# A sketch load moved to GpSimd's queue, set-up reordered, and one idle matmul removed, in a polysketch attention and GELU kernel

## Chip, cores and metric

The kernel runs on one core of a Trainium2 chip. The metric is the device time of one execution in microseconds (us). Times inside the execution are counted from the start of the profiled span. The engines are PE (matrix products, with PEld for its weight loads), DVE, ACT and POOL (GpSimd); SP only issues DMAs.

## What is computed

Attention with a polynomial sketch as its feature map, and then a two-layer block with an exact GELU over all 4352 tokens (4 batches of 1088, 4 heads of 32 channels):

```python
def phi(x):
    a = np.einsum('rd,bhsd->bhsr', S1, x)
    b = np.einsum('rd,bhsd->bhsr', S2, x)
    return np.einsum('bhsi,bhsj->bhsij', a, b).reshape(*x.shape[:-1], r * r)
q_p, k_p = (phi(q), phi(k))
kv = np.einsum('bhsf,bhsd->bhfd', k_p, v)
z = np.sum(k_p, axis=2)
num = np.einsum('bhsf,bhfd->bhsd', q_p, kv)
den = np.einsum('bhsf,bhf->bhs', q_p, z)[..., None] + 1e-06
attn_out = (num / den).astype(np.float32)
...
h = x @ w_in
g = 0.5 * h * (1.0 + erf(h * inv_sqrt2))
return (g @ w_out).astype(np.float32)
```

S1 and S2 are the two sketch matrices, 8 x 32 each. They arrive as float64, as the two weight matrices do, and are rounded to float32 on the chip: a 64-bit number is loaded as two 32-bit words, and a chain of small DVE and ACT operations puts them together.

## The kernel before

The work has two stages. The head, about the first 23 us, computes the attention of the first batch and prepares the first pieces of the weights. From there on the block's two layers run over nine chunks of tokens (eight of 512, and one of the 64 tokens left over of each batch), with the attention of the later batches woven in between. PE carries that second stage.

The order is written out by hand. A loop at the end of the text (lines 1122 to 1128) ties each instruction to the one before it on the same engine, so every engine executes in the order of the source. What an engine does early in the text it does early in time, and an instruction that waits holds up all that follow on its engine.

The steps at the start that matter here:

- **Loads of the sketches.** Lines 187 to 189 issue two DMAs from ACT's queue, S1 and then S2, into the upper and the lower half of one small tile, raw_SR (16 rows). Line 190 then loads ACT's activation table.
- **Other loads.** SP issues, in this order, the keys of batch 0 in two halves (line 192: heads 0 and 2, then 1 and 3), the first queries (193), the values in two halves (195), remainders (197) and the first weights (198 to 200).
- **Set-up on POOL.** Lines 222 to 226 and 235, 236: the identity (make_identity, two operations), a mask for the heads (mask4), a bias (below), and constants for the values' remainder.
- **Rounding of the sketches.** Lines 853 to 859: ACT and DVE turn raw_SR into SR_heads. Its parts are recorded at lines 260, 268, 273, 279 (which reads below), 287, 292 and 302.
- **PE's start.** Line 852, keep_busy(3): three products of zeros by zeros whose result nobody reads. Then, each as recorded: key_turn(0, 0), four transposes of keys against the identity (line 333); keep_busy(1) of 128 columns (line 861, recorded at 849); the transpose of SR_heads (line 319); key_turn(0, 1), four more (333).
- **After the sketches' transpose.** DVE writes S12 and sT (320, 322), POOL spreads sT into Srep (325). Then DVE transposes the queries (query_turn(0), line 519), key_features multiplies keys by S12 on PE (373), and ACT and DVE or POOL make the features k_p (386 to 390). expand_products multiplies the queries by Srep (534). kv_first sums the products of k_p and the values on PE (417).

A product of float32 by float32 shows up in the records as two matmuls, so keep_busy(1) is two.

Of the kernel before, what the change touches and what calls it, by code (L numbers as in the profile page):

```python
# [16 lines left out]
def kernel(  # L17
# [18 lines left out]
    pe, dve, act, pool, sp = nc.tensor, nc.vector, nc.scalar, nc.gpsimd, nc.sync  # L36
    B, H, S, D = q.shape
    R = S1.shape[0]
# [32 lines left out]
    def work_bank():  # L71
        return work_banks()[:, 0]
# [4 lines left out]
    def hidden_bank():  # L77
        return hps.tile([128, CW], FP, name="h_ps")
# [68 lines left out]
    def landing(dst, wide):  # L147

        if wide:
            rows, n = dst.shape  # L150
            if n == 512:

                if not half_block:
                    half_block.append(block())
                    r = half_block[0][:, 0:2]
                else:
                    r = half_block.pop()[:, 2:4]
                raw[dst.name] = r.rearrange("p a b -> p (a b)").rearrange("p (n two) -> p n two", two=2)
            elif n == 256:
                raw[dst.name] = small(U32).rearrange("p (n two) -> p n two", two=2)  # L160
            else:
                raw[dst.name] = big.tile([rows, n, 2], U32, name=f"raw_{dst.name}")
            return raw[dst.name].rearrange("p n two -> p (n two)")
        return dst

    def words(a):

        return (a, 1) if a.dtype == FP else (a.bitcast(U32), 2)
# [15 lines left out]

    S_dst = landing(SR, S1.dtype != FP)

    for i, s in enumerate((S1, S2)):
        s, e = words(s)
        act.dma_start(out=S_dst[i * R:(i + 1) * R, :], in_=s)
    nc.scalar.preload_act_table_set("gelu_and_others")  # L190
    for r in range(2):
        load_main(sp, "k", 0, slice(r, H, 2))
# [26 lines left out]
    ident = big.tile([128, 128], FP, name="ident")  # L219
    mask4 = big.tile([128, H], FP, name="mask4")  # L220
    below = big.tile([128, 1], FP, name="below")
    make_identity(nc, ident)
    pool.memset(mask4, 0.0)
    for h in range(H):
        pool.memset(mask4[h * D:(h + 1) * D, h:h + 1], 1.0)
    pool.memset(below, -896.0 * 2.0 ** 23)

    kz = [big.tile([128, 128], FP, name=f"kz{b}") for b in range(B)]

# [87 lines left out]
    def sketches():  # L317
        ps = work_bank()
        pe.transpose(ps[:, :2 * R], in_=SR_heads.rearrange("r h d -> r (h d)"), identity=ident[:2 * R, :2 * R])
        dve.tensor_mul(out=S12, in0=ps[:, None, :2 * R].broadcast_to([128, H, 2 * R]),  # L320
                       in1=mask4[:, :, None].broadcast_to([128, H, 2 * R]))
        dve.tensor_copy(out=sT, in_=ps[:, :2 * R])
        for i in range(2):
            src = sT[:, 0:R, None] if i == 0 else sT[:, None, R:2 * R]
            pool.tensor_copy(out=Srep[:, i], in_=src.broadcast_to([128, R, R]))
# [27 lines left out]
    def key_turn(b, r, ps, copy, midway=lambda: None):  # L353
        kT[r] = transposed(ps, "kT", [four_tokens("k", b, h, c) for h in (r, r + 2) for c in range(NCH)], copy, midway)
# [491 lines left out]
    def keep_busy(n, ps, cols=256):  # L846
        for i in range(n):
            noughts = [nc.const_aps.tensor(0.0, [128, m], FP) for m in (128, cols)]
            pe.matmul(ps[:, CW - cols:], lhsT=noughts[0], rhs=noughts[1], start=True, stop=True)  # L849

    bank = work_bank()
# [6 lines left out]
    r.signs()  # L858
    r.product_for_heads(SR_heads)
    key_turn(0, 0, hidden_bank(), by_act)  # L860
    keep_busy(1, bank, 128)
    sketches()
    key_turn(0, 1, hidden_bank(), by_act)
    query_turn(0)
# [294 lines left out]
```

## Time and profile before

| | us |
|---|---|
| median of 3 runs | 263.99 |
| lowest and highest of them | 263.94, 264.26 |
| the profiled execution's own time | 264.42 |
| its span, first to last instruction | 262.6 |
| PE busy | 257.3 (98% of the span) |
| POOL, DVE, ACT busy | 163.8, 151.3, 116.7 |

The profiled execution has 1.8 us around its span and is 0.43 us above the median of the three runs. PE is busy for 98% of the span and makes up 93% of the chain of work that ended last. The 40 slices of the page are 6.6 us each, so everything that the change touches lies in the first of them, and there PE stands at 8 tenths and POOL at 3. The page alone can't tell what happens there; the timeline and the chain of waits of the first 24 us can.

### The profile page before, as it was taken

To read this page: it belongs to the slowest core of one execution; us is meant where nothing else is said; L and a number is where in the kernel's file an instruction comes from. 1 tells how busy PE (TensorE), PEld (TensorE's weight loads), DVE (VectorE), ACT (ScalarE), POOL (GpSimd) and SP (SyncE) were. 2 spreads that over 40 slices of the span, in tenths; PEclk is the share of its full clock that TensorE was granted. 3 is DMA by queue.
4 is the path that set the end of the run, shared out by engine and by line. 5 is a ranking of instruction groups with operands and counts; after the bars stand their busy time and mean duration, and the time that the engine had idled before them with its cause. 6 is when DMAs were issued, how large, how long until landed. Compare 5 with 4: busy or idle time off the path is not lost.

```text
span 262.6 us, 5749 instructions
## 1 busy us (share of the span) xinstructions
PE 257.3 (98%) x2329; PEld 132.3 (50%) x2329; DVE 151.3 (58%) x307; ACT 116.7 (44%) x227; POOL 163.8 (62%) x173
## 2 busy tenths in 40 slices
PE   8999999999999999999999999999999999999994
PEld 6844444344454554444444455444444444445794
DVE  2885878969697996591267957450647042600240
ACT  3674777442635334543434334533362335433441
POOL 3403006899968676687767766867778676877200
PEclk9999999999999999999999999999999999999999
DMA  7479648730001101002000010011000100010020
GB/s 207 131 211 365 147 102 209 213 78 13 0 2 17 25 4 28 13 2 40 2 0 2 0 29 15 2 24 16 2 0 13 31 4 0 12 31 0 2 40 20
DMA packets 29530, 13.48 MB, mean 51 GB/s; under 512 B 21824, under 2 KB 27712, under 8 KB 29504
## 3 DMA queue, kind: packets, MB, share of 16 engines
q1 hardware_dynamic: 29472, 13.12, 20.2%
q8 instruction: 18, 0.29, 0.5%
q14 instruction: 8, 0.07, 0.1%
q10 hardware_dynamic: 32, 0.00, 0.0%
HBM read 10.88 MB, written 2.23 MB: 50 GB/s over the span
## 4 chain that ended last, share of the span: by engine, by line
PE 93%; DVE 3%; ACT 1%; issue 1%; POOL 1%; DVEq 0%
PE h_ps L683 43%; PE o_ps L768 33%; PE o_ps L819 5%; PE w_ps L816 3%; PE w_ps L617 2%; PE w_ps L428 1%; PE w_ps L849 1%; PE w_ps L568 1%; PE o_ps L417 1%; PE h_ps L333 1%; PE w_ps L935 1%; DVE q_pT L546 0%; PE w_ps L534 0%; DVE x_tok L656 0%; DVE w_out L297 0%
## 5 line engine op out<-in xcount | busy, mean ns | idle before, releaser
L683 PE MATMUL h_ps<-xT,w_in 128*64 128x512 f32 (+3 forms) x516 | 138.7, 577 | 0.0
L690 ACT ACTIVATE block<-h_ps 128x512 f32<-128x512 f32 (+1 forms) x128 | 73.0, 570 | 121.6 <-PE h_ps L683 115.1
L768 PE MATMUL o_ps<-block,w_out 128*64 128x256 f32 x224 | 57.8, 380 | 0.3 <-DVE sums L789 0.3
L683 PEld LDWEIGHTS h_ps<-xT,w_in 128*64 128x64 f32 (+1 forms) x516 | 42.0, 143 | 30.1 <-issue 11.4
L733 POOL TENSOR_TENSOR bits_low<-block 128x512 f32<-128x512 f32 x28 | 35.6, 1273 | 28.6 <-ACT block L690 28.6
L768 PEld LDWEIGHTS o_ps<-block,w_out 128*64 128x64 f32 x224 | 30.2, 137 | 38.8 <-issue 25.8
L734 POOL TENSOR_TENSOR bits_a<-block 128x512 f32<-128x512 f32 x28 | 35.7, 1277 | 14.0 <-ACT block L690 14.0
L735 POOL TENSOR_TENSOR bits_e<-bits_a,block 128x512 f32<-128x512 f32 x28 | 36.3, 1297 | 2.2
L736 POOL TENSOR_TENSOR bits_m<-block,bits_e 128x512 f32<-128x512 f32 x28 | 35.8, 1280 | 2.2
L784 DVE TENSOR_TENSOR sums<-o_ps,sums 64x512 f32<-64x512 f32 x8 | 5.5, 682 | 41.3 <-ACT sums L781 23.6
L768 PE MATMUL o_ps<-bits_low,small 128*64 128x256 f32 x112 | 29.2, 383 | 0.0
L768 PE MATMUL o_ps<-block,small 128*64 128x256 f32 x112 | 29.1, 383 | 0.0
L768 PE MATMUL o_ps<-bits_a,small 128*64 128x256 f32 x112 | 29.0, 382 | 0.0
L768 PE MATMUL o_ps<-bits_m,w_out 128*64 128x256 f32 x112 | 28.8, 380 | 0.0
L580 DVE STREAM_TRANSPOSE w_ps<-w_ps 128x512 f32<-128x512 f32 (+1 forms) x7 | 4.8, 691 | 38.5 <-PE w_ps L568 38.5
L768 PEld LDWEIGHTS o_ps<-block,small 128*64 128x64 f32 x112 | 14.7, 137 | 18.4 <-issue 10.0
L768 PE MATMUL o_ps<-bits_e,small 128*64 128x256 f32 x112 | 17.2, 385 | 0.0
L819 PE MATMUL o_ps<-g,w_out 128*128 128x512 f32 x32 | 16.4, 600 | 0.5 <-DVE w_out L297 0.5
L768 PEld LDWEIGHTS o_ps<-bits_m,w_out 128*64 128x64 f32 x112 | 15.4, 137 | 0.0
L768 PEld LDWEIGHTS o_ps<-bits_a,small 128*64 128x64 f32 x112 | 14.9, 137 | 0.0
L768 PEld LDWEIGHTS o_ps<-bits_low,small 128*64 128x64 f32 x112 | 14.7, 137 | 0.0
L690 ACT ACTIVATE g<-h_ps 128x512 f32<-128x512 f32 x16 | 9.5, 594 | 7.7 <-PE h_ps L683 7.1
(181 smaller groups left out, 297.2 us busy)
## 6 DMA issues: line engine op xcount, KB each, us to landing
out_dram<-oT SPq DMA_DIRECT2D x26, 64.0 KB, 2.2
block<-in_moe_w_in_dram SPq DMA_DIRECT2D x3, 512.0 KB, 7.1
block<-in_moe_w_out_dram SPq DMA_DIRECT2D x3, 512.0 KB, 13.0
k<-in_k_dram SPq DMA_DIRECT2D x12, 128.0 KB, 3.0
v<-in_v_dram SPq DMA_DIRECT2D x12, 128.0 KB, 3.3
q<-in_q_dram SPq DMA_DIRECT2D x24, 64.0 KB, 2.2
k<-in_k_dram SPq DMA_DIRECT2D x2, 256.0 KB, 2.8
q<-in_q_dram SPq DMA_DIRECT2D x2, 256.0 KB, 4.2
```

The source lines that it names most:

```text
L580: dve.transpose(out=tok, in_=ps[:, :, :H2])
L617: pe.matmul(banks[h * D:(h + 1) * D, s, i * N:(i + 1) * N], lhsT=(kz[b] if b else kz_first)[rows, h * D:(h + 1) * D], rhs=f[rows, h // 2, ...
L683: pe.matmul(ps[rows, :W], lhsT=w[:, rows], rhs=xT[n][:, :W], start=True, stop=True)
L690: act.activation(out=g_of[n, fi][:, :W], in_=ps[:, :W], func=ACT.Gelu)
L733: pool.tensor_sub(out=s[3], in0=a11, in1=a21)
L734: pool.tensor_add(out=s[1], in0=a21, in1=a22)
L735: pool.tensor_sub(out=s[2], in0=s[1], in1=a11)
L736: pool.tensor_sub(out=s[4], in0=a12, in1=s[2])
L768: pe.matmul(acc[n][bank][half * 64:(half + 1) * 64, col:col + HW], lhsT=fixed, rhs=moving, start=opens and e == 0 and name in "4715", stop ...
L784: dve.tensor_add(out=C[lo, 1], in0=a1[lo], in1=C[lo, 0])
L816: pe.matmul(o_of[n][i][:, :128], lhsT=g[:, i * 128:(i + 1) * 128], rhs=w_tile(w_out_sb, fi), start=first, stop=final)
L819: pe.matmul(o_of[n], lhsT=w_tile(w_out_sb, fi), rhs=g, start=first, stop=final)
```

## The change

Three edits in the set-up and one in PE's order come with it:

```diff
-    for i, s in enumerate((S1, S2)):
+    for i, (s, eng) in enumerate(((S1, pool), (S2, act))):
         s, e = words(s)
-        act.dma_start(out=S_dst[i * R:(i + 1) * R, :], in_=s)
+        eng.dma_start(out=S_dst[i * R:(i + 1) * R, :], in_=s)
     nc.scalar.preload_act_table_set("gelu_and_others")
...
     below = big.tile([128, 1], FP, name="below")
+    pool.memset(below, -896.0 * 2.0 ** 23)
     make_identity(nc, ident)
     pool.memset(mask4, 0.0)
     for h in range(H):
         pool.memset(mask4[h * D:(h + 1) * D, h:h + 1], 1.0)
-    pool.memset(below, -896.0 * 2.0 ** 23)
...
     key_turn(0, 0, hidden_bank(), by_act)
-    keep_busy(1, bank, 128)
     sketches()
```

S1 is now issued by POOL, as the first instruction of its order in the kernel's text; S2 becomes the first DMA that ACT issues. On POOL the bias below is written ahead of the identity instead of behind the mask. On PE the two matmuls of keep_busy(1) between the keys' first transposes and the sketches' transpose are gone.

## The prediction

> **What bounds the kernel now.** I read the chain of waits first, over the whole span and then for the first 24 us in order of time, to see whether the edited place lies on it at all. It does: this stretch of PE's order has no other engine in it.
>
> ```profile
> 0.77 2.90 PE w_ps L849 x6
> 3.67 0.97 PE h_ps L333 x4
> 4.65 0.43 PE w_ps L849 x2
> 5.07 0.21 PE w_ps L319
> 5.29 1.06 PE h_ps L333 x4
> 6.35 0.02 issue
> 6.37 0.59 ACT kT L335
> 6.96 0.04 issue
> 7.01 0.67 PE h_ps L373 x32
> 7.68 1.05 PE w_ps L534 x32
> 8.72 0.63 PE o_ps L417 x16
> ```
>
> The columns are start, length, and what. The reader is to see that the idle product (L849 x2) stands on the chain with 0.43 us, between work that somebody needs, and that the chain passes from it without a gap to the sketches' transpose (L319). Next, the timeline of the same microseconds, for what the other engines do beside it, when the sketches arrive, and what could be late when PE is early.
>
> ```profile
> 3.53 0.23 ACT L260 ACTIVATE bits_low<-raw_SR 16x32 f32<-16x32 uint32 x1 [0.57 <-DMA raw_SR<-in_S_dram]
> 4.37 0.28 DVE L302 TENSOR_TENSOR SR_heads<-bits_m,bits_e 16x128 f32<-16x128 f32 x1
> 5.00 0.18 PEld L319 LDWEIGHTS w_ps<-ident,SR_heads 16*128 16x128 f32 x1 [0.22 <-issue]
> 6.40 0.71 DVE L519 STREAM_TRANSPOSE qT<-q 128x512 f32<-128x512 f32 x1 [0.70 <-DMA q<-in_q_dram]
> 7.27 1.29 DVE L390 TENSOR_TENSOR k_p<-a_t,o_ps 128x512 f32<-128x512 f32 x2 [0.16 <-ACT a_t L389]
> 8.67 0.57 PEld L417 LDWEIGHTS o_ps<-sums,k_p 128*64 128x64 f32 x16 [0.40 <-issue]
> ```
>
> Columns: start, length, engine, line, operation, and in brackets the idle time before and what ended it. The sketches land just before 3.53, and SR_heads is complete at 4.37 + 0.28 = 4.65. That is the very moment at which the keys' transposes end on the chain (4.65). The idle product stands in a place in which PE would otherwise have waited only for the hand-over. DVE later waits 0.70 us for the queries' DMA, which lands at 6.40, and from there it is busy until 7.11 and idle for only 0.16 us before k_p. That small number will decide.
>
> Third, the groups of the loads and of the keys' transposes.
>
> ```profile
> L189 ACTq DMA_DIRECT2D raw_SR<-in_S_dram x2: 283/444/605, 0.7 to 1.4; - x2
> ```
> ```profile
> L333 PE MATMUL h_ps<-ident,k x8: 421/422/473, 3.6 to 5.9; 128*128 128x128 f32 x8
> L333 PE MATMUL w_ps<-ident,q x4: 272/273/329, 11.6 to 12.0; 128*128 128x128 f32 x4
> ```
>
> Least, median and greatest ns of one, then first and last start. The second sketch's DMA is issued at 1.4, behind the first (605 ns on the queue), and landing is at 3.5: 2.1 us. The same transpose costs 422 ns until 5.9 us and 273 ns later: PE is slow at the start, whatever the page's clock digits say.
>
> [...] No DMA from POOL is in this trace. [...] Here DVE is idle from about 1.0 us to 3.5 us; only three memsets of 0.1 us lie near the issue. [...]
>
> **Part 1: S2 alone on ACT's queue.** S2 moves from second to first, so its issue moves from 1.4 to 0.7 and its landing to no later than 3.53 - 0.6 = 2.9. The table load (1.68, 1.28 us) moves up by the same issue, to end near 2.5. ACT next waits for the sketches, so this earns nothing by itself.
>
> **Part 2: S1 on POOL's queue.** Lowest cost: small transfers of this trace take 1.5 to 1.7 us from SP's issue to landing (rows of the outputs and of q_rem)[...]. Higher: the second sketch took 2.1 us amid the keys' traffic[...]. [...] I take 3.25, which is 0.3 earlier than now. Then SR_heads is there at 4.35, before PE asks for it. The wait of DVE L268 and ACT L260 is still for two DMAs. Behind them on DVE is the rounding, and PE's L319 waits for that; behind L319 stands the second half of the keys.
>
> **Part 3: POOL's order.** The DMA stands ahead of the rest. [...]everything on POOL slides by about 0.7 us: the identity from 1.30 to 2.0 or 2.1 with the memset of below ahead of it (0.10), the mask from 1.89 to 2.6, the remainder's constants from 2.66 to 3.4. They are wanted at 3.53 (L333), 5.39 (L320) and 9.68. The bias below comes right behind the DMA and is wanted at 3.81. The cost is nothing, covered by PE's first idle products and the keys' load; the cover is gone when POOL is held more than 3.53 - 1.30 = 2.2 us. SP's queue is passed by nothing, so k, q and v are issued when they were.
>
> **Part 4: the idle product.** Two matmuls, 0.43 us of chain, go. With SR_heads at 4.35, L319 begins 0.43 earlier. With SR_heads at 4.65 as now and some 0.1 us to hand over to PE (its k_p wait ends at 8.67, 0.11 after 8.56), it begins at 4.76 instead of 5.00 and earns 0.24. Now what is late next. L333 and the copy of kT move with L319, L373's second group to about 6.6. On DVE, k_p stands behind the queries' transpose, which starts with q's landing at 6.40 and ends at 7.11. So k_p goes from 7.27 to 7.13, and no further: 0.14 us. L534 needs qT too, at 7.11, and would start near 7.2, which leaves PE waiting some 0.25 us ahead of L417, whose start is set by k_p: 8.67 - 0.14. Behind it the kernel hangs on PE and DVE in turn, without a DMA, to 23.17, and from there PE runs back to back, so what L417 earns arrives at the end.
>
> **The sum.** -0.43 for the product, +0.29 given back at q's landing: -0.14. Against the profiled execution that is 264.42 - 0.14 = 264.28, its span 262.46. That execution was 0.43 above the median, so I set the prediction against the median: 263.99 - 0.14 = 263.85. A measurement of this kernel can tell from no change about 0.2%, that is 0.53 us.
>
> **Rivals.** (a) *The full 0.43 arrives*: 263.56. For it: the chain puts all of it on PE. Against it: q's landing, which no edit moves; k_p would need another order on DVE. (b) *Nothing, or a little lost*: S1 lands between 3.6 and 4.3 and PE idles where the product stood, so the edit has only exchanged an idle product for idle time. With S1 at 3.9, L319 starts 0.37 after 4.76, 0.13 late: 264.12. (c) *Slower: S1 late on POOL's queue.* The sketches' landing gates DVE's rounding, and through L319 all of PE. Break-even is a landing 0.24 later than now, at 3.77; from there each ns is lost, since the slack before k_p is none in that direction. It decides against the change from 3.77 + 0.53 = 4.3, which is 3.6 us after issue, against 2.5 that I take. [...] For it: there is no POOL DMA in the trace[...]. Against: POOL and DVE are empty. (d) *The clock.* PE's idle gap ahead of L319, if S1 is late, could put off the release. The work from 7.01 to 9.4 would run at 422/273 of its time: (0.67 + 1.05 + 0.63) x 0.55 = 1.3 and more: 265.3. [...] Against: on my forecast PE has other work at once. (e) *Faster by over 0.53 us*: only a release of the clock that comes earlier could do it, and nothing in the edits calls for it.
>
> **How the numbers follow.** Forecast (0 to 0.25 gained) 0.38; (a) 0.10; (b) 0.14; (c) 0.24; (d) 0.07; (e) 0.07. Within 0.2% are the forecast, (a) and (b): 0.62. Slower are (c) and (d): 0.31. Faster is (e): 0.07. The range goes from 263.4, just under (a), to 265.1, past the middle of (c), and leaves out (e), (d) and the far end of (c), about 0.2 in all. The likeliest case's own range is 263.7 to 264.0.
>
> **What would show it.** Right: a POOL DMA near 0.73 of 0.6 to 1.0 us, raw_SR's readers starting by 3.3, L319 near 4.57, q's transpose still at 6.40, k_p at 7.13, L417 near 8.53, and PE idle ahead of it. Wrong: rounding that starts after 3.77, an identity after 3.5, transposes of 422 ns beyond 6.3 us, or a gap on PE ahead of L319 longer than 0.1 us. The prediction fails if S1's landing is over 0.3 us off my 3.25 to the late side and as far again, or if q lands at another time.

## The result, and the profile after

The changed kernel takes 270.48 us (median of 4 runs, 269.95 to 271.06), the kernel before 264.02 (median of 4, 263.94 to 264.26). The ratio is 1.0242, with a 95% interval of 1.0229 to 1.0255: 2.4% slower, where I had forecast 0.14 us faster and a range that ended at 265.1. The profiled execution took 269.95 us, with a span of 268.2, against 264.42 and 262.6 before: 5.6 us more span.

Executions of one kernel fall into groups some us apart here, and in the twelve traces of this case the time goes with the moment at which PE's clock comes to full speed and stays there (by 6.4 us: 263.4 to 264.8; at 10.1: 265.3; at 20 or later: 270.0 to 271.2), so the sections below count the runs of each group.

First the chain of waits of the changed kernel, in order of time: start, length, and what.

```profile
1.25 3.05 DMA raw_SR<-in_S_dram
...
5.50 0.23 PE w_ps L319
5.73 0.60 PE h_ps L333 x4
...
6.99 0.67 PE h_ps L373 x32
7.65 1.90 PE w_ps L534 x32
9.55 1.00 PE o_ps L417 x16
...
28.55 1.10 PE o_ps L819 x2
```

In the kernel before, the last of these lines is:

```profile
23.17 1.10 PE o_ps L819 x2
```

Two things are to be seen. The sketches' DMA from POOL is now the head of the chain, and PE's transpose L319 starts at 5.50 instead of 5.00. Yet L534 starts at 7.65, as before (7.68): the half microsecond has been won back by the keys' second transposes, which took 1.06 us and take 0.60, because the clock was released at 4.29 in this run, and at 6.28 in the traced run of the kernel before. The loss begins behind that, where no edit was made. L534 takes 1.90 instead of 1.05, L417 1.00 instead of 0.63, and so on to L819, the start of PE's long run: 28.55 instead of 23.17. Those 5.4 us are all but 0.2 of the 5.6.

Next the timeline of the start, with what each instruction had waited for.

```profile
1.25 0.70 POOL L189 DMA_DIRECT2D raw_SR<-in_S_dram  x1 [0.81 <-POOLq L1142]
2.29 0.29 POOL masks.py:199 TENSOR_SCALAR_AFFINE_SELECT ident<-ident 128x128 f32<-128x128 f32 x1
3.57 0.98 PE L333 MATMUL h_ps<-ident,k 128*128 128x128 f32 x4
4.33 0.17 DVE L268 TENSOR_SCALAR bits_e<-raw_SR 16x32 uint32<-16x32 uint32 x1 [3.37 <-DMA raw_SR<-in_S_dram]
5.50 0.23 PE L319 MATMUL w_ps<-ident,SR_heads 16*128 16x16 f32 x1 [0.95 <-DVE SR_heads L302]
```

POOL's DMA is recorded from 1.25, not from 0.73 as I had put it; its instruction takes 0.70 us, and the data are there at 4.31, 2.4 us after that. The identity is ready at 2.58, well ahead of its use. PE stands idle for 0.95 us ahead of L319.

Last, the windows of the changed kernel: bounds, then length and busy time with counts for PE, PEld, DVE, ACT and POOL, and then the granted clock, the DMA share and GB/s.

```profile
7.00:7.70 0.70, 0.70 (x40) 0.66 (x48) 0.45 (x1) 0.33 (x2) 0.42 (x1) 1.00 0.91 259
7.70:8.30 0.60, 0.60 (x16) 0.48 (x24) 0.60 (x2) 0.38 (x2) 0.20 (x1) 0.51 0.96 317
...
20.60:21.20 0.60, 0.60 (x2) 0.51 (x2) 0.60 (x3) 0.56 (x2) 0.00 (x0) 0.50 1.09 292
21.20:22.00 0.80, 0.80 (x4) 0.62 (x4) 0.77 (x3) 0.03 (x1) 0.00 (x0) 0.90 0.90 307
```

The clock drops to half at 7.71. It is 0.90 on average over the last line's 0.80 us, so the half clock ends 0.16 us into it (0.16 x 0.5 + 0.64 = 0.72 = 0.90 x 0.80), at 21.36. It lasts 13.65 us in all. PE has work in nearly all of it, and that work is the head's. The products themselves say the same. Here is L534 by its source line, changed kernel first, then the kernel before (least, median and greatest ns):

```profile
L534 PE MATMUL w_ps<-qT,Srep x64: 598/629/681, 7.6 to 18.5; 32*64 32x256 f32 x64
```
```profile
L534 PE MATMUL w_ps<-qT,Srep x64: 373/375/427, 7.6 to 14.0; 32*64 32x256 f32 x64
```

The products are needed beside the clock's column, which reads 1.00 also ahead of the first record of the clock. In this profile that record begins at 4.29, and of the keys' eight transposes (L333, 3.6 to 6.0 us) the slowest takes 447 ns and the quickest 272. The moments of release given below are those at which the clock's record in a trace begins.

### The profile page after: what moved, and what is told of

It is laid out like the page before. It is cut to its first block, busy times and chain, and to the rows that moved or that the text cites. A ratio compares the mean times of both kernels' runs of the same rounds, so it can differ in the third digit from the quotient of the medians.

```text
span 268.2 us, 5746 instructions
## 1 busy us (share of the span) xinstructions
PE 261.8 (98%) x2327; PEld 135.5 (51%) x2327; DVE 151.4 (56%) x307; ACT 116.7 (44%) x227; POOL 164.9 (61%) x174
## 4 chain that ended last, share of the span: by engine, by line
PE 92%; DVE 3%; DMA 1%; ACT 1%; issue 1%; POOL 1%; DVEq 0%; ACTq 0%; POOLq 0%
PE h_ps L683 42%; PE o_ps L768 32%; PE o_ps L819 5%; PE w_ps L816 3%; PE w_ps L617 1%; PE w_ps L428 1%; PE w_ps L534 1%; PE o_ps L417 1%; PE w_ps L568 1%; DMA raw_SR<-in_S_dram 1%; PE w_ps L934 1%; PE w_ps L333 0%; DVE q_pT L546 0%; PE h_ps L664 0%; PE h_ps L635 0%
## 5 line engine op out<-in xcount | busy, mean ns | idle before, releaser
L819 PE MATMUL o_ps<-g,w_out 128*128 128x512 f32 x32 | 16.4, 600 | 0.5 <-DVE w_out L297 0.5
```

Of the source, the lines that this page charges most:

```text
L819: pe.matmul(o_of[n], lhsT=w_tile(w_out_sb, fi), rhs=g, start=first, stop=final)
```

## The experiments

Three theories. A: TensorE's clock; PE's idle gap ahead of L319, and the product that used to fill part of it, decide whether the clock is released early and stays. B: the idle product alone does. C: the POOL DMA and what it holds up.

**e1: the idle product alone taken out.**

```diff
     key_turn(0, 0, hidden_bank(), by_act)
-    keep_busy(1, bank, 128)
     sketches()
```

> The kernel before with the idle product of 0.43 us alone taken out; both sketches stay on ACT's queue. Theory A (the change loses through TensorE's clock: PE stands idle while it waits for a late sketch, and the clock goes or stays at half until about 21 us): the gap ahead of the sketches' transpose is only about 0.1 us, so the clock still holds, and the time is 263.7 to 264.0. Theory B (the idle product itself is what opens the clock, gap or no gap): 269 to 271. Theory C (the loss is in the POOL DMA and what it holds up): 263.7 to 264.0 as well.

264.14 us (median of 22) beside 264.18 of the kernel before (57 runs), ratio 1.0010 [0.9996, 1.0024]. But the runs are not alike: 15 lie at 263.6 to 264.4, with a median of 263.99, five at 265.7 and two at 269.5 and 269.8. Of the kernel before, 52 lie at 263.7 to 264.7, with a median of 264.15, four at 265.9 and one at 269.9. So without the product the bulk's median is 0.16 us lower, and seven of 22 runs, not five of 57, come out above 265. Neither A (all near 264) nor B (all at 270) as written: the product shifts the odds.

The trace of a run from the bulk:

```profile
4.75 0.23 PE L319 MATMUL w_ps<-ident,SR_heads 16*128 16x16 f32 x1 [0.19 <-DVE SR_heads L302]
5.31 0.70 DVE L519 STREAM_TRANSPOSE qT<-q 128x512 f32<-128x512 f32 x1
7.93 0.66 PE L417 MATMUL o_ps<-sums,k_p 128*64 128x33 f32 x16
```

L319 is at 4.75, 0.25 earlier, as worked out (4.76). But the missing product is not what put it there: in the traces of e5 and e9 below, which have the product, L319 starts at 4.79 and 4.74 and L417 at 7.97 and 7.93. In all three the clock was released at about 4.3 (4.29, 4.26, 4.36) instead of 6.28, and at full clock the product takes 0.39 us instead of 0.64. The queries were there at 5.31 at the latest, not at 6.40, and L417 starts 0.77 us earlier than in the kernel before. About half of that is lost again by L819 (22.76 instead of 23.17); at 11.7 the chain of this run goes through the DMA of the first weights:

```profile
6.61 5.10 DMA small<-in_moe_w_in_dram
11.71 0.02 issue
11.73 0.82 DVE bits_e L268
```

**e2: the changed kernel with the product put back** (the one line of the diff above, added again).

> The changed kernel with the idle product put back: S1 still from POOL, POOL's order as changed. The rounded sketches should be there at 5.45 as in the changed kernel, so PE's gap shrinks from 0.95 to about 0.5 us. Theory A: if a gap of 0.5 us is still too long for the clock, 269 to 271; if it holds, L319 is 0.5 us later than before and the time 264.3 to 264.6. Theory B: 264.3 to 264.6. Theory C: 270 as in the changed kernel.

Twelve of 20 runs at 264.5 to 264.8 (median 264.63), one at 266.4, seven at 270.2 to 271.4. So whether the clock is released in time differs from run to run. The trace is of one of the seven (270.27): PE stands idle for 0.41 us ahead of L319, and the clock is first released at 20.06. The twelve, with POOL's DMA in place, cost 0.48 us over the bulk of before.

**e3: the changed kernel with two idle products.**

```diff
     key_turn(0, 0, hidden_bank(), by_act)
+    keep_busy(2, bank, 128)
     sketches()
```

> The changed kernel with two idle products in the place of the one that was taken out, so that PE is at work until about 5.3 us when the late sketches arrive at 5.45. Theory A: no gap, the clock is released near 6 us and stays, and what is left is the half microsecond by which the sketches are later: 264.3 to 264.7. Theory B: the same. Theory C: about 270, since the POOL DMA is there as in the changed kernel.

264.64 us, and all 19 runs between 264.55 and 264.96. The DMA on POOL, its late landing (SR_heads at 5.58) and POOL's new order are all there, and 5.8 of the 6.5 us are gone. C is out but for half a microsecond, which the interval against before (ratio 1.0010 [0.9997, 1.0022]) does not tell from nothing.

Theory A as written has a hole here, though. I expected no gap, and the trace has one:

```profile
5.63 0.23 PE L319 MATMUL w_ps<-ident,SR_heads 16*128 16x16 f32 x1 [0.89 <-DVE SR_heads L302]
```

The clock was released at 3.69 in this run, so the two products took 0.61 us and were over at 4.73. PE's idle time is nearly that of the changed kernel (0.95), and the clock stays. So a gap of this length does not by itself lose it: with the two products beside it none of e3's 19 runs lies above 265, and with none of them, at a gap of 0.95, all four of the changed kernel's lie at 269.9 or above.

Before, e1, e2 and the changed kernel are the four combinations of a sketch in time or late with the product or without it. At 269 us and above lie 1 of 57, 2 of 22, 7 of 20 and 4 of 4 of their runs. Neither edit alone does that to most runs; both together did it to all four.

**e4: PE's gap without any POOL DMA.** The kernel before without the product, and in the sketches' rounding:

```diff
     r.mantissas()
+    for t in (*kz, kz_first):
+        dve.memset(t, 0.0)
     r.signs()
```

> The kernel before without the idle product and with both sketches on ACT's queue, but five memsets of 128x128 on DVE in the middle of the sketches' rounding, which make the rounded sketches about 0.7 us late: PE gets the changed kernel's gap without any DMA on POOL. Theory A: the transposes and products of the head run at half clock until about 20 us, 269 to 271. Theory C: 264.3 to 264.7, since nothing is on POOL's queue.

265.32, 269.35, 270.19 and 270.36 us. PE is idle for 0.57 us ahead of L319 in the trace (of the quickest of them, in which the clock is released at 10.1 us). No run of the four is near 264, and three are at 269 or above, where e1, without the added delay, has 2 of 22: the gap brings the loss with both sketches on ACT's queue.

**e5: the bias ahead of the identity alone** (the memset of below moved up, nothing else).

> The kernel before with one edit alone: POOL writes the bias ahead of the identity. All theories: nothing waits for either, the identity is done at 1.4 instead of 1.3 and wanted at 3.5, so the time is that of the kernel before, 263.9 to 264.3.

264.14 us against 264.18 (12 and 43 runs), ratio 1.0000 [0.9989, 1.0010], no run above 265. The reordering costs nothing that can be measured.

**e6: the same filling, over a small part of the array.**

```diff
     key_turn(0, 0, hidden_bank(), by_act)
+    for i in range(2):
+        noughts = [nc.const_aps.tensor(0.0, [32, m], FP) for m in (64, 128)]
+        pe.matmul(bank[:64, 384:], lhsT=noughts[0], rhs=noughts[1], start=True, stop=True)
     sketches()
```

> The changed kernel with two idle products in the gap again, as many matmuls and columns as in the filled one, but over 32 rows and 64 columns of the array instead of 128 by 128. If the clock gate goes by the time for which PE has an instruction at work, PE is as busy as in the filled kernel and all runs are at 264.5 to 264.7. If it goes by how much of the array works, an eighth of the array is no help and most runs are at 269.5 to 271, as in the changed kernel.

270.53, 271.23, 271.37 and 271.41 us, where all 19 runs of e3 are below 265. The windows of e3 and then of e6, in the columns above:

```profile
0.00:8.00 8.00, 6.25 (x94) 4.70 (x102) 2.58 (x13) 3.33 (x8) 3.51 (x18) 1.00 0.74 207
```
```profile
0.00:8.00 8.00, 7.22 (x59) 5.19 (x59) 2.05 (x11) 2.88 (x5) 3.52 (x18) 1.00 0.69 201
```

By its records PE is busy for 6.25 of the first 8 us in e3 and for 7.22 in e6; the changed kernel has 6.19. Part of that difference is the clock itself, at half of which a product takes longer (L534: 629 ns in the changed kernel, 375 in the kernel before). The chain of e6 is the stronger evidence: it shows no gap on PE from 0.78 to 21.51, and its products stay slow all that time (32 of L534 take 1.94 us, where the kernel before has 1.05); the clock is released for the first time at 22.60:

```profile
4.75 1.04 PE w_ps L863 x4
...
8.91 1.94 PE w_ps L534 x32
```

So in this trace over 20 us of PE at work without a gap did not by themselves bring the release. Idle products over 128 by 128 in this place keep the kernel near 264.6; as many matmuls with as many columns over 32 by 64, which took longer here (1.04 us against 0.61), do not.

**e7: idle time in the place of the product**, with L319 near its old time: as e4, with memsets of kz[1:3] only.

> The kernel before without the idle product, both sketches on ACT's queue, and two memsets of 128x128 on DVE inside the rounding, so that the sketches' transpose starts near 5.0 as before: PE stands idle for the 0.4 us in which it multiplied zeros. Clock theory: the work is the same, at the same times, so the best runs are at 264.0 to 264.3; but a larger share than the 5 in 57 of before lies above 265, between that of the kernel with the product taken out (7 of 22) and that of the one with the longer gap (4 of 4). Rival (the product is only filler and the clock is a matter of S1's late DMA): 264.0 to 264.3 with no more runs above 265 than before.

Ten of 22 runs at 263.2 to 264.2, five at 264.9 to 265.1, seven at 268.8 to 270.0. The first two lie 0.6 to 0.7 us below e1's first two, the third between 0.8 below and level with e1's third, so 12 of 22 belong to the two upper ones. That is far more than before has (1 of 43 in the runs beside them), which refutes the rival; that it is more than e1 has (7 of 22) fits the clock theory, but so many runs cannot tell the two shares apart. In the traced run, one of the ten, the clock was released at 5.77, the keys' first transposes lasted until 4.74, and L319 started at 4.87, so that PE stood idle for 0.13 us and not for 0.4. That the lower group lies below before wasn't expected; in the trace DVE's last product for w_out (L297) waits for nothing, where it stands 0.53 us idle in the kernel before.

**e8: the product moved** from ahead of the sketches' transpose to between the two groups of L373.

> The kernel before with the idle product moved from ahead of the sketches' transpose to between the two groups of L373, where PE waits some 0.2 us for a copy of kT. Clock theory: PE has as much to do as before in the first 8 us, so few runs lie above 265, and the sketches' transpose starts 0.24 earlier, of which 0.1 to 0.2 reach the end: median 263.85 to 264.0 where before has 264.1 to 264.2. Rival (where the product stands matters, not that it is there): as without the product, a third of the runs above 265.

Seven of 14 runs at 263.9 to 264.8, seven at 270.2 to 271.6. My expectation failed: what matters is not that there is a product in the first 8 us, but where. At its old place it stands between transposes over the whole array, at the new one among small products; that this is the reason is not shown, as the trace is of one of the seven lower runs (264.37, clock released at 5.01).

**e9: POOL's later spreading of the sketches (lines 468 to 478) moved up**, from 21.5 us, where it is on the chain of before, to 12.4, where POOL stands idle.

```diff
     load_rest()
+    spread_sketches()
     w_out = [Rounding(w, beside=b) for w, b in zip(w_out_sb[:2], w_in)]
...
-    at(11, spread_sketches)
```

> The kernel before with POOL's spreading of the sketches (lines 468 to 478) moved up to where POOL stands idle, from 21.5 us to about 13.3. Theory from the chain of the kernel before and of the one with 0.4 us of idle PE: the last product of w_out on DVE (L297) stands 0.53 us for POOL's S_ab and no longer does, so the first of the long run of PE (L819) starts at about 22.7 instead of 23.17: 263.5 to 263.8, below both kernels. Rival: DVE's x_tok operations at 13 to 15 us are held up by the same POOL work instead, and the time is 264.0 to 264.5.

263.87 us (median of 22) against 264.36 (36 runs), ratio of the runs compared 0.9987 [0.9973, 1.0001]. Its median is the lowest of all versions, 6.6 us under the changed kernel's, but against before the interval just reaches 1. The reason that I gave is refuted: L297 still stands idle.

```profile
22.17 0.42 DVE L297 TENSOR_TENSOR w_out<-bits_m,bits_e 128x256 f32<-128x256 f32 x1 [0.52 <-DVE bits_e L292]
22.74 1.10 PE L819 MATMUL o_ps<-g,w_out 128*128 128x512 f32 x2 [0.52 <-DVE w_out L297]
```

S_ab, to which the profile of before put the wait down, is done by 13.4 here, and the same half microsecond remains. What causes it stays open, and so does whether e9 gains anything.

**e10: two idle products in the kernel before** (keep_busy(1, ...) to keep_busy(2, ...)).

> The kernel before with two idle products instead of one ahead of the sketches' transpose. Clock theory: PE's array has more to do in the first 8 us, so next to no run lies above 265 (of the kernel before 6 of 100 did), and the sketches' transpose starts up to 0.43 us later, less where the clock is released earlier: 264.2 to 264.6. Rival (a product more or less doesn't matter to the clock once one is there): as many runs above 265 as before.

264.27 us beside 264.36, all 14 runs between 263.6 and 265.0, while five of the 36 runs of before beside them were above 265.2. One more product costs nothing that can be measured. None of the 14 runs is in the upper groups, as the clock theory has it, but at before's share of 5 in 36 that would come about by chance in about one series of eight ((31/36)^14 = 0.12, an estimate), so this is not shown.

## Why the prediction was wrong

- **What bounds the kernel; the chain.** Right: the place lies on PE's chain, and SR_heads and the keys' transposes ended together.
- **Part 1, S2 alone on ACT's queue.** Not contradicted; with S1 late it earns nothing.
- **Part 2, S1 on POOL's queue.** The first step that failed, by size. I took 3.25 for the landing; it is 4.31. Of the 1.06 that is missing, 0.52 is the start (1.25 instead of 0.73; 1.26 in e2 and 1.25 in e3), and the rest, 0.54, the way from there to the landing: 3.06 us, where I had taken 2.5, of which only the 2.1 of ACT's second DMA stood in a trace. From start to landing the two queues differ by 0.9 here (3.06 against 2.16, ACT's second DMA in the chain of e4). POOL is held for 0.70 us, as much as the 0.7 by which I let its order slide; that was an estimate with no trace behind it, so the agreement is luck.
- **Part 3, POOL's order.** Right in what it cost: identity at 2.58 and bias at 2.08, both ahead of use, and e5 shows no cost. The identity is 0.5 us later than I had it (2.0 or 2.1), by the DMA's later start.
- **Part 4, the idle product.** L319 in e1 came as worked out, and the bulk's 0.16 us is near the 0.14 of the sum, but the way there was luck: with an early release L319 comes as early with the product in place (4.74 in e9), and q's landing isn't fixed at 6.40 and didn't hold e1 up, while the first weights' landing did.
- **The product as filler only.** The step that cost the case. I wrote that it "stands in a place in which PE would otherwise have waited only for the hand-over", and priced its absence in time on the path. With a late sketch its absence costs the clock as well: at 269 us or above lie 4 of 4 runs of the changed kernel, which has no product there, 7 of 20 with the product put back (e2), and none of 19 with two (e3). I named the clock as rival (d), with 0.07, priced at 1.3 us because I let the delay end at 9.4, and 265.3. Measured: 13.65 us at half clock and 5.4 us lost, since the clock, taken back at 7.71, came again only at 21.36. Rival (b), which took idle time in the product's place to cost next to nothing, has the same fault.
- **Rival (c)**, a late S1, has the right cause and a small part of the sum: S1 at 4.31 would have cost 0.54 by its formula (4.31 - 3.77), and e3 and the twelve of e2, which have the late S1 and the clock, cost 0.5. The two rivals belong together: the late landing makes the gap (0.95 us), and the gap, with no product in it, cost the clock in all four runs.

In the trace of the changed kernel the record of the clock has full clock for 3.41 us from 4.29, half for 13.65 from 7.71, and full again for 245.76 from 21.36; in that of the kernel before it has full clock for 256.00 us from 6.28. What sets these moments and lengths, and so why the runs of one kernel fall into groups, the traces do not show.

In the changed kernel and in e1, which has no product either but its sketches in time, the clock was released at the same moment, 4.29. Here is the stretch from there to 7.71, the changed kernel first:

```profile
4.29:7.71 3.42, 2.39 (x79) 1.79 (x85) 2.32 (x9) 1.93 (x6) 1.02 (x3) 1.00 0.95 264
4.29:7.71 3.42, 3.15 (x103) 2.26 (x101) 2.50 (x8) 1.88 (x6) 1.38 (x4) 1.00 0.96 259
```

PE is busy for 2.39 us of it in the first and for 3.15 in the second, with as much work over the whole array in both (L333: 0.91 and 0.92). At its end the first loses the clock and the second keeps it. In e3, released at 3.69, the clock stays, though from 4 to 6 us PE is busy for 1.11 us, hardly more than the 1.05 of the changed kernel; but there the two idle products put 0.61 us of work over the whole array beside the transposes. So of two traces with as much array work the one with the longer gap lost the clock, and of two with nearly the same gap the one with less array work did. That is one trace of each, and which of the two decides is not shown. The release goes the same way: e10, with no gap on PE ahead of L319, has it at 6.40, and e2, with a gap of 0.41 us there, not before 20.06. And the changed kernel lost its clock though PE had been at work for 2.39 of the 3.41 us before.

What stays open: which work of PE's brings the release. Two products over the whole array kept the clock and e6's did not, but in e4's trace the clock was released at 10.1 us amid products of 64 by 64 and 32 by 64, which in the changed kernel brought no release at that time.

## What to carry to other kernels

An idle matmul in a start-up isn't free filling: before one is taken out, or anything is made late ahead of PE in the first microseconds, ask what it may do to PE's clock (here 0.95 us of idle time with no product in it went with the loss of the clock, and 0.89 us with two products did not), and compare the ns of one product at the same shape before and after rather than PE's busy share. Price a lost clock by the time for which it stays lost: here 13.65 us at half clock, nearly the whole of the head that was left. And take many runs, since such an edit can leave the usual time alone and change how often the clock is lost. A tiny load that heads a dependency chain was better off on ACT's queue here: from POOL it landed 0.8 us later than as the second DMA on ACT's.

## What was not expected of the hardware

- With two idle products over 32 by 64, PE had no gap from 0.78 to 21.51 us and its clock stayed at half until 22.60; with two over 128 by 128 and a gap of 0.89 us, the clock was released at 3.69 and stayed.
- The clock was taken back at 7.71, 3.41 us after it had been released, and then kept at half for 13.65 us, though PE was busy for 2.39 us of the 3.41 and for 13.52 of the 13.65.
- POOL's first DMA was recorded 0.5 us after the other queues' first (1.25 against 0.74), with nothing ahead of it in the kernel's text.
- DVE's L297 stands idle for 0.53 us in the kernel before, for 0.52 in e9, and for none in e7, which has two more DVE instructions early in its order. In e9 the POOL operation to which before's profile puts the wait is long done, so that operation is not needed for it.
